# Another order for the opening of a fused attention and mixture-of-experts kernel

## The chip, the cores and the metric

The kernel runs on one core of one Trainium2 chip. The metric is the device time of one execution in microseconds (us), the median of several runs. TensorE multiplies matrices and also transposes tiles (a matmul with an identity matrix), VectorE and ScalarE do element-wise work, GpSimd (POOL) helps with setup and some subtractions, and SyncE (SP) issues DMAs.

## The reference

Three stages follow each other. The change lies in the first.

```python
q_bits = (einsum('bhsd,dk->bhsk', q, proj) > 0)     # 6 bits for each row; k_bits alike
mask = q_bucket[..., :, None] == k_bucket[..., None, :]
scores = scale * q @ k.T                            # 2 batches x 8 heads, 768 x 768, head size 64
scores = where(mask, scores, -1e9); scores -= max(scores, -1)
attn = exp(scores); attn /= sum(attn, -1) + 1e-9
x = (attn @ v), heads side by side                  # 1536 tokens x 512
x = (h * tanh(softplus(h))) @ w_out, h = x @ w_in   # 512 -> 2048 -> 512
out = one of 8 experts for each token, by cosine similarity: relu(x @ w1[e]) @ w2[e] * gate
```

## The kernel before, in words

There are 16 heads, numbered 0 to 15 through both batches. Each head goes through the same steps, and the later heads run side by side in a software pipeline whose step g does one sixth of a head. The opening, from the first load to the start of that pipeline, has an order of its own, which is written out by hand as the text `PRO`: each line names a step and its head. `run_all` walks over the lines and issues the instructions of each. A dependency is added between neighbours on each engine, so each engine runs its instructions in the order in which the lines issue them, and an instruction that must wait holds all that stand behind it on its engine.

The steps of the lines:

- `load_kq` (L276) loads k and q of two heads, one DMA of 384 KB each; `load_v` (L368) loads v of two heads, two DMAs of 192 KB. SP issues these in the opening, in program order. The line `kq 4` is the load of heads 4 and 5.
- `hi n` (L286): ScalarE rounds k and q of head n to a first float16 part, 768 columns. `lo n s` (L292): VectorE takes the second float16 part of k (s=0) or q (s=1). `lo_pool n` (L297, L301): the same for a whole head, with ScalarE scaling in place and GpSimd subtracting.
- `x n p`: twelve 128x128 transposes on TensorE (L254), into two PSUM tiles of pool p (s or o). `cx n 0` and `cx n 1` (L256) copy these two tiles to SBUF; the last letter names the engine, a for ScalarE and d for VectorE.
- `dup n` (L307) copies the first parts into the mask tile `kq` of the head. `args n` (L320): twelve small matmuls that project k and q on 6 directions, into PSUM (with `o`, into the pool that is also used by `x 1` and `m 1`). `bits n`, three times (L330, L331, L332): VectorE sums the projections and writes +-16384 by their sign into the mask tile; so a matmul of the mask tiles of q and k gives a large number where the buckets agree.
- `m n p` and `cm n 0`, `cm n 1`: twelve transposes of the mask tile and the copies of the results, like x and cx. They read all that dup and bits write.
- `max_unit n j c` finds the maximum of each row. With c=0: one matmul of 512 columns (L382) into a PSUM tile of the pool `ps_m`, and one VectorE reduction (L383). With c=1: two matmuls of 256 columns (L386), one reduction (L387). That pool has two buffers, so a unit's matmul waits until VectorE has read the unit before the last. For head 0 each unit with c=0 first issues one filler matmul (L230) into the same tile. A head needs nine units.
- `max_end n` (L395, L396): the two small VectorE operations that end the maxima. `rows_t n` (L403) transposes the maxima to a row, six small transposes, and `rows_in n` (L407) copies the row into the mask tile's 97th row.
- `score_unit n t`: four matmuls (L422 of q and k; L424 of the mask with the row of maxima) and one exponential on ScalarE (L427).
- `warm k` and `warm_s k` issue k filler matmuls (L230), whose results nobody reads.
- `pv` (L444), later in the pipeline, multiplies the exponentials by v.

The tiles that hold the first and second parts (`ka`) have two buffers, the mask tiles `kq` three, and the tiles that the loads write two, for two heads each.

Of the kernel before, what the change touches and what calls it, by code (L numbers as in the profile page):

```python
# [76 lines left out]
lo 1 0  # L77
m 0 s
lo 1 1
dup 1 d  # L80
cm 0 0 a
hi 2
cm 0 1 d
x 1 o
max_unit 0 0 0
kq 4
max_unit 0 1 1
cx 1 0 a
lo_pool 2
max_unit 0 3 0  # L90
cx 1 1 a
max_unit 0 2 0
warm_s 2
args 1 o 0
warm_s 5
args 1 o 1
bits 1
max_unit 0 1 0
max_unit 0 3 1
x 2 s  # L100
bits 1
cx 2 0 a
dup 2 a
max_unit 0 4 0
bits 1
max_unit 0 5 0
max_unit 0 5 1
m 1 o
cx 2 1 a
max_end 0  # L110
max_end 0
cm 1 0 a
max_end 0
rows_t 0
rows_in 0
args 2 m
bits 2
bits 2
bits 2
cm 1 1 a  # L120
hi 3
lo_pool 3
score_unit 0 0
max_unit 1 0 0
hi 4
# [22 lines left out]
class Attn:  # L148
# [364 lines left out]
    def run_all(self, bs, hook=None):  # L513

        seq = [(b, h) for b in bs for h in range(H)]
        N = len(seq)

        self.load_v(0, 0)
        self.load_kq(0, 2)
        act, dve = self.nc.scalar.copy, self.nc.vector.tensor_copy  # L520
        Z, pools, copies, its = self.Z, dict(s=self.ps_s, o=self.ps_o, m=self.ps_m), dict(a=act, d=dve), {}
        for line in PRO:
# [38 lines left out]
        for n in range(N):  # L561
            for name, at in AT.items():
# [10 lines left out]
                elif name in GAP:  # L573
                    d = GAP[name]
# [15 lines left out]
        for g in range(G0, TEND + 1):  # L590
            n, t = divmod(g, NJ)
            m, j = divmod(g + MXL, NJ)
# [848 lines left out]
```

## Time and profile before

| what | us |
|---|---|
| median of 3 runs | 677.6 (677.41 to 677.87) |
| the profiled execution | 676.44 |
| its span, first to last instruction | 674.5 |
| granted TensorE clock, mean | 0.998 of full speed |
| VectorE busy | 480.2 (71%) |
| ScalarE busy | 483.8 (72%) |
| GpSimd busy | 167.8 (25%) |

The times of rows are microseconds from the start of the span. A row of a timeline gives the start, how long the row lasted, the engine, the line of the kernel, the operation, the written tile, the read tile, and how many instructions were merged (x2). In brackets is how long the engine had been idle before it, and which instruction released it by the profile. Instructions of an engine overlap a little at their ends. PE is TensorE's matmuls, PEld its weight loads, DVE is VectorE and ACT ScalarE.

### The profile page before, as it was taken

The page shows a single profiled execution, that of the slowest core. Times are in us where ns is not written, and L with a number is a line of the kernel's source. Part 1 is how long each engine was busy: PE and PEld are TensorE (multiplying, and loading weights), DVE is VectorE, ACT ScalarE, POOL GpSimd, SP SyncE. Part 2 cuts the span into 40 slices and gives each one's busy share as a digit, 9 for nine tenths or more (in the row PEclk, how much of TensorE's full clock was granted, in tenths as well). Part 3 has the DMA queues.
Part 4 walks back from the last instruction along what each step waited for, and adds up shares of the span by engine and source line. Part 5 has one row for each costly group of instructions (what it writes and reads, how often), then busy time and mean ns, then how long its engine had stood idle before and what let it go on. Part 6 is the DMA issues. An engine that isn't in the chain of part 4 may idle for free. (4 is left out here: it accounts for less than half of the span.)

```text
span 674.5 us, 10665 instructions
## 1 busy us (share of the span) xinstructions
PE 657.5 (97%) x3946; PEld 376.9 (56%) x3946; DVE 480.2 (71%) x784; ACT 483.8 (72%) x735; POOL 167.8 (25%) x226
## 2 busy tenths in 40 slices
PE   7899999999999999999999999999999999999995
PEld 4555555555555544444444544445477777667772
DVE  6868999999988559999575676755565655556620
ACT  5657788787776889899799788887754655555530
POOL 4123132131231223222253242532522011101011
PEclk9999999999999999999999999999999999999999
DMA  7165675958663323457033030310355999989700
GB/s 234 33 152 115 181 180 118 235 135 181 158 124 88 87 63 103 115 178 207 15 85 89 1 126 13 84 31 1 127 187 179 258 280 309 293 249 262 179 23 22
DMA packets 119772, 92.72 MB, mean 137 GB/s; under 512 B 86788, under 2 KB 99076, under 8 KB 119714
## 3 DMA queue, kind: packets, MB, share of 16 engines
q1 hardware_dynamic: 111442, 80.65, 45.5%
q0 software_dynamic: 2240, 6.31, 3.3%
q10 hardware_dynamic: 6032, 5.01, 2.4%
q8 instruction: 33, 0.54, 0.4%
q14 instruction: 25, 0.20, 0.1%
HBM read 63.44 MB, written 14.24 MB: 115 GB/s over the span
## 5 line engine op out<-in xcount | busy, mean ns | idle before, releaser
L820 PE MATMUL h<-xx,wi 128*128 128x512 f16 x576 | 131.3, 379 | 0.7 <-DVE w L905 0.6
L879 PE MATMUL x<-wo,g 128*128 128x512 f16 x576 | 131.2, 379 | 0.0
L444 PE MATMUL o<-p,vn 128*65 128x384 f32 (+3 forms) x272 | 108.7, 486 | 0.3 <-ACT su L469 0.3
L427 ACT ACTIVATE p<-s 128x768 f32<-128x768 f32 x96 | 76.9, 806 | 31.5 <-PE s L424 30.1
L915 POOL TENSOR_TENSOR g<-w,g 128x512 f16<-128x512 f32 x47 | 57.7, 1228 | 149.2 <-ACT g L914 89.8
L879 PEld LDWEIGHTS <-g 128*128 128x128 f16 x576 | 56.3, 98 | 68.0 <-POOL g L915 0.3
L820 PEld LDWEIGHTS <-wi 128*128 128x128 f16 x576 | 56.1, 98 | 68.0 <-issue 1.7
L1220 PE MATMUL y<-b,hh 128*128 128x512 f16 (+1 forms) x384 | 84.2, 379 | 0.0
L1206 PEld LDWEIGHTS <-a 128*128 128x128 f16 x768 | 75.0, 98 | 5.6 <-issue 0.5
L383 DVE TENSOR_REDUCE mx<-ms 128x1 f32<-128x512 f32 x96 | 65.3, 686 | 8.1 <-PE ms L382 7.4
L1206 PE MATMUL h<-xt,a 128*128 128x240 f16 x672 | 70.3, 266 | 0.2 <-DVE hh L1213 0.2
L1220 PEld LDWEIGHTS <-hh 128*128 128x128 f16 (+1 forms) x384 | 43.7, 114 | 37.6
L921 DVE SCALAR_TENSOR_TENSOR w<-w,u 128x512 f32<-128x512 f32 x47 | 32.5, 691 | 45.3 <-ACT u L912 45.3
L704 DVE SCALAR_TENSOR_TENSOR b<-st,b 128x1024 f16<-128x1024 f32 x28 | 33.1, 1222 | 28.4 <-ACT b L703 28.4
L444 PEld LDWEIGHTS o<-p,vn 128*65 128x65 f32 (+1 forms) x272 | 42.3, 163 | 18.2 <-issue 8.0
L1226 POOL DMA_INDIRECT out_dram<-o,row x16 | 16.1, 1006 | 143.4 <-ACT o L1225 129.8
L704 DVE SCALAR_TENSOR_TENSOR a<-st,a 128x1024 f16<-128x1024 f32 x28 | 34.3, 1224 | 19.5 <-ACT a L703 19.1
L900 DVE SCALAR_TENSOR_TENSOR t<-t,u 128x512 f32<-128x512 f32 x47 | 40.6, 863 | 9.9 <-ACT t L927 9.9
L424 PE MATMUL s<-tm 97*128 97x384 f16 x192 | 47.0, 325 | 0.0
L422 PE MATMUL s<-tx 128*128 128x384 f16 x192 | 46.8, 325 | 0.0
L1225 ACT ACTIVATE o<-y,row 128x512 f32<-128x512 f32 (+1 forms) x16 | 11.0, 686 | 42.6 <-PE y L1220 22.8
L387 DVE TENSOR_REDUCE mx<-ms 128x2 f32<-128x512 f32 x48 | 32.9, 686 | 9.8 <-PE ms L386 9.1
(207 smaller groups left out, 1070.3 us busy)
## 6 DMA issues: line engine op xcount, KB each, us to landing
st<-in_moe_w_dram SPq DMA_DIRECT2D x32, 1024.0 KB, 6.3
stg<-in_moe_w_in_dram SPq DMA_DIRECT2D x16, 512.0 KB, 4.4
stg<-in_moe_w_out_dram SPq DMA_DIRECT2D x16, 512.0 KB, 4.2
xs<-zrow SPq DMA_DIRECT2D x15, 257.0 KB, 6.7
vn<-in_v_dram SPq DMA_DIRECT2D x16, 192.0 KB, 4.2
rb<-rd SPq DMA_DIRECT2D x14, 192.0 KB, 3.4
xr<-row SPq DMA_DIRECT2D x2, 1024.0 KB, 5.6
kq<-in_k_dram ACTq DMA_DIRECT2D x5, 384.0 KB, 4.4
```

Source lines behind the costliest of these rows:

```text
L383: nc.vector.tensor_reduce(z["mx"][:, j, 0:1], s, axis=AX.X, op=ALU.max)
L422: nc.tensor.matmul(s[:, c, :], kq[:, 0, ts], kq[:, 1, c * HS : (c + 1) * HS], start=True, stop=False)
L424: nc.tensor.matmul(s[:, c, :], m[0:97, 0, ts], m[0:97, 1, c * HS : (c + 1) * HS], start=False, stop=True)
L427: nc.scalar.activation(p[:, 0:S].rearrange("p (c n) -> p c n", c=2), s, AF.Exp, scale=2.0**-11)
L444: nc.tensor.matmul(o, self.vn(b, h, t), z["p"][t][:, cs], start=(t == 0), stop=(t == NJ - 1))
L704: nc.vector.scalar_tensor_tensor(lo, src, sc, hi, op0=ALU.mult, op1=ALU.subtract)
L820: self.nc.tensor.matmul(h, self.wi[wu][:, k, fs], x[:, k, xs], start=(i == 0), stop=(i == 3 * NKT - 1))
L879: nc.tensor.matmul(x2[r], gf[:, gu, rs], self.wo[wu][:, f, :], start=(f == 0 and gu + wu == 0), stop=(f == NF1 - 1 and gu == 1))
L900: nc.vector.scalar_tensor_tensor(t1, t1, 0.75, u1, op0=ALU.add, op1=ALU.mult)
L915: nc.gpsimd.tensor_tensor(g[G - 1][:, 1, :], p1, g[G - 1][:, 0, :], op=ALU.subtract)
L1206: nc.tensor.matmul(h[:, v, :], W[0][wu][:, k, fs], xt[e][:, xu * NKT + k, :], start=(i == 0), stop=(i == 3 * NKT - 1))
L1220: nc.tensor.matmul(y[s][0 : CS[s].stop - CS[s].start], hs[F // 2][:, hu, F % 2, CS[s]], W[1][wu][:, F, :], start=(F == 0 and hu + wu == 0) ...
```

## The change

The two loads of k and q of heads 2 and 3 are issued ahead of the two of v. In the opening, head 1's second copy `cx 1 1` goes ahead of head 2's split `hi 2` on ScalarE, and both ahead of `lo_pool 2`; head 1's `dup` on VectorE moves behind the first two maxima units. The seven fillers around head 1's projections become three, and both halves of these projections follow each other. The maxima of head 0, head 1's bits, head 1's mask transposes `m 1`, and head 2's transposes `x 2` are interleaved in another order: all three bits operations come before unit "4 0", `m 1` is before it on TensorE and `x 2` behind it. The split of head 3 (`hi 3`, `lo_pool 3`) is issued earlier, ahead of the last maxima of head 0, where it stood right before the first scores.

```diff
--- before.py
+++ after.py
@@ -77,49 +77,48 @@
 lo 1 0
 m 0 s
 lo 1 1
-dup 1 d
 cm 0 0 a
-hi 2
 cm 0 1 d
 x 1 o
 max_unit 0 0 0
 kq 4
 max_unit 0 1 1
 cx 1 0 a
+cx 1 1 a
+hi 2
+dup 1 d
 lo_pool 2
 max_unit 0 3 0
-cx 1 1 a
 max_unit 0 2 0
-warm_s 2
+warm_s 3
 args 1 o 0
-warm_s 5
 args 1 o 1
 bits 1
+dup 2 a
 max_unit 0 1 0
+bits 1
 max_unit 0 3 1
+bits 1
+hi 3
+m 1 o
+max_unit 0 4 0
+lo_pool 3
+cm 1 0 a
 x 2 s
-bits 1
+max_unit 0 5 0
 cx 2 0 a
-dup 2 a
-max_unit 0 4 0
-bits 1
-max_unit 0 5 0
 max_unit 0 5 1
-m 1 o
-cx 2 1 a
 max_end 0
 max_end 0
-cm 1 0 a
 max_end 0
+cx 2 1 a
 rows_t 0
 rows_in 0
+cm 1 1 a
 args 2 m
 bits 2
 bits 2
 bits 2
-cm 1 1 a
-hi 3
-lo_pool 3
 score_unit 0 0
 max_unit 1 0 0
 hi 4
@@ -515,8 +514,8 @@
         seq = [(b, h) for b in bs for h in range(H)]
         N = len(seq)
 
+        self.load_kq(0, 2)
         self.load_v(0, 0)
-        self.load_kq(0, 2)
         act, dve = self.nc.scalar.copy, self.nc.vector.tensor_copy
         Z, pools, copies, its = self.Z, dict(s=self.ps_s, o=self.ps_o, m=self.ps_m), dict(a=act, d=dve), {}
         for line in PRO:
```

## Rows read from the trace of the kernel before

**Rows 1.** The page, busy time: engine, us, share of the span, instructions.

```profile
PE 657.5 (97%) x3946; PEld 376.9 (56%) x3946; DVE 480.2 (71%) x784; ACT 483.8 (72%) x735; POOL 167.8 (25%) x226
```

**Rows 2.** Busy time by stretch: us, engines, then TensorE's granted clock, DMA share, GB/s.

```profile
5.00:10.00 5.00, 4.53 (x57) 3.15 (x56) 4.18 (x14) 2.27 (x3) 1.32 (x13) 1.00 0.89 262
...
18.00:19.00 1.00, 0.37 (x7) 0.19 (x4) 0.91 (x3) 0.93 (x2) 0.00 (x0) 1.00 0.19 66
...
20.00:25.00 5.00, 4.22 (x33) 2.39 (x32) 4.77 (x12) 4.97 (x8) 1.79 (x2) 1.00 0.00 0
...
35.00:40.00 5.00, 5.00 (x27) 2.44 (x27) 2.80 (x5) 3.33 (x5) 0.59 (x1) 1.00 0.79 205
```

**Rows 3.** Timeline of VectorE in the opening: start, us, instruction, idle time before.

```profile
9.44 0.36 DVE L307 COPY kq<-ka 128x768 f16<-128x768 f16 x1
...
11.36 0.68 DVE L387 TENSOR_REDUCE mx<-ms 128x2 f32<-128x512 f32 x1
...
14.81 0.38 DVE L330 TENSOR_REDUCE ag<-ar 128x72 f32<-128x216 f32 x1 [1.45 <-PE ar L320]
...
16.42 0.19 DVE L331 TENSOR_SCALAR kq<-ag 128x72 f16<-128x72 f32 x1
...
17.18 0.19 DVE L332 TENSOR_SCALAR kq<-ag 128x72 f16<-128x72 f32 x1
...
17.28 0.69 DVE L383 TENSOR_REDUCE mx<-ms 128x1 f32<-128x512 f32 x1
...
17.88 0.68 DVE L387 TENSOR_REDUCE mx<-ms 128x2 f32<-128x512 f32 x1
```

**Rows 4.** Timeline of TensorE's matmuls in the opening.

```profile
8.74 0.83 PE L254 MATMUL psm<-ident,kq 128*128 128x128 f16 x12 [0.24 <-DVE kq L332]
...
9.41 0.83 PE L254 MATMUL psx<-ident,ka 128*128 128x128 f16 x12
...
12.26 0.38 PE L382 MATMUL ms<-tm 96*128 96x512 f16 x1
...
12.47 0.49 PE L230 MATMUL warmed<-ones 128*128 128x384 f16 x2
...
14.47 0.31 PE L320 MATMUL ar<-pj,tx 128*128 128x18 f16 x6 [0.29 <-ACT tx L256]
...
14.63 0.32 PE L230 MATMUL ms<-ones 128*128 128x384 f16 x1
...
14.79 0.38 PE L382 MATMUL ms<-tm 96*128 96x512 f16 x1
...
19.03 0.50 PE L403 MATMUL tm<-ident,m 128*1 128x128 f16 x6 [0.66 <-DVE m L396]
...
20.18 0.48 PE L424 MATMUL s<-tm 97*128 97x384 f16 x2
...
23.51 0.38 PE L382 MATMUL ms<-tm 96*128 96x512 f16 x1 [0.57 <-DVE mx L387]
```

**Rows 5.** Timeline of ScalarE in the opening.

```profile
9.27 0.80 ACT L256 COPY tm<-psm 128x768 f16<-128x768 f16 x1 [1.21 <-PE psm L254]
...
11.45 0.84 ACT L286 ACTIVATE ka<-kq 128x768 f16<-128x768 f32 x1 [1.38 <-DVE mx L383]
...
13.62 0.79 ACT L256 COPY tx<-psx 128x768 f16<-128x768 f16 x1
...
20.34 0.84 ACT L297 ACTIVATE kq<-kq 128x768 f32<-128x768 f32 x1
...
21.09 0.79 ACT L427 ACTIVATE p<-s 128x768 f32<-128x768 f32 x1
```

**Rows 6.** SP's issue, its landing (last number, DMA view), v's first matmul.

```profile
6.03 0.47 SPq L276 DMA_DIRECT2D kq<-in_q_dram  x1
...
kq<-in_q_dram SPq DMA_DIRECT2D x1, 384.0 KB, 5.3
...
28.67 0.81 PE L444 MATMUL o<-p,vn 128*65 128x384 f32 x2
```

## The prediction

> **What bounds the kernel now.** I read the engine totals first. TensorE is busy for 97% of the span [rows 1], so a change of order pays only where TensorE stands idle, and nearly all of its idle time that this change can reach lies in the opening. Then I read the busy time by stretch [rows 2]: from 35 us on TensorE is busy in all of the five microseconds, while from 20 to 25 us it has 4.22 of 5.00 and VectorE 4.77. After that I read the timelines of the two engines, one beside the other. The reader is to see there who waits for whom. At 23.51 us a matmul of the maxima waited 0.57 us for a VectorE reduction [rows 4], because the two PSUM buffers of the maxima come free only when VectorE has read them. So between 20 us and the full stretch VectorE sets the pace, and it starts that work when the first head's row of maxima is done. That row is a chain: nine reductions, the two small operations that end them, six transposes on TensorE that start at 19.03 us, a copy, and the matmuls at 20.18 us that add the row to the first scores [rows 4]. Whatever moves these two times moves all that follows by as much, since from there on the order on each engine is the same, TensorE's and VectorE's work is the same, and TensorE fills up. The question of the change is thus when these transposes start. Inside the chain VectorE has one large hole, 1.45 us before 14.81 us, in which it waits for the second head's projections on TensorE [rows 3].
>
> **Part one: the loads.** The k and q loads of heads 2 and 3 are issued by SP ahead of the two v loads instead of behind them. Before, the later one (q) took 5.3 us from its issue at 6.03 us to land, at about 11.3 us [rows 6]. ScalarE's split of head 2 started at 11.45 us after 1.38 us of idling [rows 5]; the view names a VectorE reduction as releaser, but the split reads nothing of it, so I take the landing for the cause. With the new order the data is there earlier by the time of the two v loads. I cost this at nothing: in the new order ScalarE reaches that split only after two copies. The copy of head 0 starts at 9.27 us [rows 5]; one copy takes about 0.73 us start to start, so the two end near 11.5 us, which is where the split started before. The v loads now have two loads of 384 KB ahead of them; at the 262 GB/s of this stretch [rows 2] these take 3 us, and v lands later by so much. The first matmul that reads v runs at 28.67 us, more than 20 us after SP's issues here [rows 6], so the cover stays. If the cover were gone, the price would be that delay, at most 3 us. The next load on SP, of heads 4 and 5, waits for the second head's split on VectorE, which is not moved: nothing. The bounds for the part are 0 and -0.1 us.
>
> **Part two: the second head's copies on ScalarE go ahead.** Now both end near 11.5 us; before, the second started at 13.62 and ended at 14.41 us [rows 5]. So the projections of head 1 no longer wait for ScalarE; they wait for their place on TensorE. The matmul of the fourth maxima unit starts at 12.26, and the first filler behind it at 12.47 [rows 4]. Three fillers at 0.16 us each (14.63 to 14.79) put the projections at 12.95. All twelve now run together: their second six started at 14.47, lasted 0.31 us and had the next matmul start 0.16 us behind them [rows 4], so twelve take 0.31 us of issue and end near 13.41. On VectorE the copy named dup of head 1 has moved into the maxima: it lasts 0.36 us, of which I count 0.27, since an operation starts some 0.09 us before the one ahead of it ends (the reduction at 17.28 lasts 0.69, and the next starts 0.60 later) [rows 3]. Its place is free at about 11.97, a reduction after 11.36. So the next two reductions run at 12.24 and 12.84, and the first bits operation of head 1 can go at 13.45. That is 1.36 us earlier than 14.81, and the hole has closed. Bounds: 1.45 us at the best, nothing if the projections come no sooner.
>
> **Part three: the other order of the maxima.** Here the gain is spent again. After the projections TensorE issues a filler and the matmul of unit "1 0" at 13.42; it takes 0.38 us, so VectorE reduces it at 13.84 (before: projections 14.47, filler 14.63, matmul 14.79 [rows 4]). The second bits operation follows 0.60 us later, at 14.44. From the second bits operation to the third there were 0.76 us with one reduction between them (16.42 to 17.18) [rows 3], so the third starts at 15.20 and ends at 15.39. Now TensorE has the twelve mask transposes of head 1 as its next work, ahead of the matmul of unit "4 0", and they read what the third bits operation wrote. They start at about 15.45 and occupy TensorE for 0.67 us (8.74 to 9.41, where two such sets follow each other) [rows 4]. Only then come the filler at 16.12 and the matmul at 16.28, which VectorE can reduce at 16.70. VectorE could have gone on at 15.30 (0.10 behind the third bits operation, as at 17.18 and 17.28 [rows 3]) and has nothing until 16.70: a new hole of 1.40 us, counted from start to start. Behind that matmul (0.22 us of issue, as from 12.26 to 12.47 [rows 4]) stand head 2's twelve transposes, again 0.67 us, from 16.50 to 17.17. The matmul of unit "5 0" is at 17.33 and its reduction at 17.75, while VectorE was free at 17.31: a second hole of 0.44 us. The last reduction starts 0.60 later, at 18.35, against 17.88 before [rows 3]. From the start of that reduction to the row's transposes were 1.15 us (17.88 to 19.03), which puts them at 19.50. From there to the matmuls with the row were 1.15 us again (19.03 to 20.18) [rows 4], so they run at 20.65. The shift is +0.47 us.
>
> **Part four: what ScalarE and GpSimd gain.** The split of head 3 and its scaling leave the place right before the first exponential for the idle time after 13 us. The scaling at 20.34 held the first exponential until 21.09 [rows 5], when its scores had been done since 20.66 (20.18 and 0.48 [rows 4]). In the new order the scores are done at 21.13, and the exponential starts then: ScalarE's delay of 0.43 us goes, and the late row uses it up. Nothing on VectorE or TensorE waited for that exponential. I take zero, with 0 and -0.4 us as the bounds. Four fillers fewer save 0.65 us of TensorE's time, but they stood in waits; zero on the path.
>
> **The sum.** -1.36 (the projections earlier, with dup's 0.27 already in it), +1.40 and +0.44 (two new holes) make +0.48 us; the single starts above, rounded at each step, give 0.47. The profiled execution took 676.44 us, 1.94 of it outside its span of 674.5, and nothing outside the span changes, so it would become 676.9. The median of the runs shown is 677.6, 1.2 us more, and the same +0.5 gives 678.1 us. The ends: if VectorE never waited in the new order, the chain would gain 1.45 less dup's 0.27, or -1.2 us; if the projections came no earlier and both holes were paid, +1.8 us.
>
> **Rivals.** What a measurement of this kernel can tell from no change is about 0.2%, or 1.36 us.
> (a) The hole closes and none opens: the mask transposes run before VectorE runs out of reductions. It would need the third bits operation to end by about 14 us, and my times say 15.39. For it speaks the 1.45 us hole, against it the strict order on TensorE. Price -1.2, 676.4 us.
> (b) The opening shifts, but the later stretch takes it back: the ScalarE time of part four turns out to matter between 20 and 27 us. For it speaks that ScalarE was busy for 4.97 of 5.00 us there [rows 2], against it that TensorE's waits there name VectorE. Price 0, 677.6 us.
> (c) The clock falls. The new order leaves TensorE idle from about 14.0 to 15.45 and from 17.9 to 19.50 us, with four fillers fewer; before, its longest waits after the first matmul were 0.66 and 0.57 us [rows 4]. If the granted clock fell to its lower level (1.2 GHz, half) by 20 us, the 4.22 us of matmul time from 20 to 25 us would become 8.44 in place of 5.00: +3.4 us for each such stretch, 681.5 us with the shift. It decides as soon as one stretch behind the holes shows a clock under 1.00. Against it: from 18 to 19 us TensorE was busy for only 0.37 us, and the clock stayed at 1.00 [rows 2]. The Trainium skill's page "TensorE: Matmul & The Clock Gate", section "What's actually happening", speaks against the change here: "the default state is throttled, and activity releases the throttle". By that rule less activity in the opening is a risk; the trace of before, at 1.00 in all stretches read, shows no change of level.
> (d) The projections come late all the same, because the 'o' buffer or a semaphore holds them: +1.8, 679.4 us.
>
> **How the numbers follow.** Forecast 0.58, (a) 0.12, (b) 0.17, (c) 0.06, (d) 0.07. Forecast and (b) are within 0.2%. Of (a) half may pass the bound, with the scatter of the runs (677.41 to 677.87), so faster gets 0.06. (c) and most of (d) pass it on the other side: slower 0.12. The rest, 0.82, is no change that can be told. The range reaches to (a) and (d), 676.3 to 679.4 us; the forecast's own range is 677.7 to 678.6.
>
> **What would show it.** Right: the first bits operation of head 1 near 13.45 us, a VectorE hole of over a microsecond before the reduction of unit "4 0" near 16.7, a smaller one before "5 0", the row's transposes near 19.5, a clock of 1.00. Wrong: transposes of the row before 19.0, or a clock under 1.00 between 15 and 25 us, or the full TensorE stretch starting no later although the row is late.

## The result, and the profile after

The changed kernel is slower. Its median is 682.43 us (680.01 to 683.50, 6 runs) against 677.67 (677.21 to 678.41, 6 runs) of the kernel before, 4.8 us more. The ratio of the runs is 1.0060, with a 95% interval of 1.0045 to 1.0076, which is 3.1 to 5.2 us. The profiled execution of the changed kernel took 682.44 us, with a span of 680.2. The forecast of 678.1 and the range up to 679.4 were wrong. The time is near that of rival (c), the fall of the clock, which was put at 681.5 us and had got a chance of 0.06.

The page shows the totals and TensorE's granted clock in 40 slices of 17 us each. TensorE's busy share is what it was [rows 1]; the new thing is the second digit of the clock, a 7. (The last digit covers the end of the span, where TensorE runs out of work.)

```profile
PE 659.2 (97%) x3942; PEld 378.4 (56%) x3942; DVE 480.7 (71%) x784; ACT 483.8 (71%) x735; POOL 168.1 (25%) x226
...
PEclk9799999999999999999999999999999999999997
```

The same row of the kernel before:

```profile
PEclk9999999999999999999999999999999999999999
```

The busy time by stretch, as in [rows 2], shows where that is (the number behind POOL is the granted clock):

```profile
12.00:16.00 4.00, 2.38 (x23) 1.18 (x22) 3.99 (x8) 3.88 (x5) 1.78 (x2) 1.00 1.00 341
...
16.00:20.00 4.00, 3.43 (x30) 2.32 (x30) 1.60 (x5) 2.87 (x4) 1.85 (x2) 0.71 0.67 222
...
20.00:24.00 4.00, 2.93 (x24) 1.72 (x25) 2.20 (x8) 0.52 (x2) 0.23 (x1) 0.50 0.00 0
...
24.00:28.00 4.00, 3.43 (x28) 2.15 (x26) 3.66 (x7) 3.28 (x5) 0.05 (x1) 0.94 0.00 0
```

From 12 to 16 us TensorE was busy for 2.38 of 4.00 us, with the clock still at 1.00. In the next four the mean fell to 0.71, it was 0.50 (the level of 1.2 GHz) from 20 to 24 us, and it came back before 25 us. Taken together, that is some 7 us at the lower level.

The timeline of TensorE's matmuls answers to [rows 4]:

```profile
14.06 0.38 PE L385 MATMUL ms<-tm 96*128 96x256 f16 x2
...
16.28 0.84 PE L253 MATMUL psm<-ident,kq 128*128 128x128 f16 x12 [1.84 <-DVE kq L331]
...
17.12 0.38 PE L381 MATMUL ms<-tm 96*128 96x512 f16 x1
...
17.34 1.19 PE L253 MATMUL psx<-ident,ka 128*128 128x128 f16 x12
...
18.64 0.63 PE L381 MATMUL ms<-tm 96*128 96x512 f16 x1
...
21.07 0.80 PE L402 MATMUL tm<-ident,m 128*1 128x128 f16 x6 [1.36 <-DVE m L395]
...
22.73 0.85 PE L423 MATMUL s<-tm 97*128 97x384 f16 x2
...
26.84 0.38 PE L381 MATMUL ms<-tm 96*128 96x512 f16 x1 [0.57 <-DVE mx L386]
```

The twelve mask transposes of head 1 waited 1.84 us for the third bits operation. Behind them the matmul of unit "4 0" still took 0.38 us, but head 2's twelve transposes took 1.19 in place of 0.83, and a maxima matmul 0.63. That is the fall; it came behind the first wait, while TensorE was at work again, and before the second wait. The row's transposes waited another 1.36 us and ran at 21.07, the matmuls with the row at 22.73. The matmul that had waited at 23.51 us [rows 4] waited for the same reduction at 26.84: 3.33 us later. From there to the end of the attention stage nothing is gained or lost: the first matmul of the next stage starts at 240.69 us in place of 237.38, which is 3.31 us later.

The timeline of VectorE, as in [rows 3]:

```profile
11.17 0.69 DVE L382 TENSOR_REDUCE mx<-ms 128x1 f32<-128x512 f32 x1 [0.49 <-PE ms L381]
...
13.87 0.38 DVE L329 TENSOR_REDUCE ag<-ar 128x72 f32<-128x216 f32 x1
...
14.87 0.65 DVE L330 TENSOR_SCALAR kq<-ag 128x72 f16<-128x72 f32 x1
...
15.44 0.68 DVE L386 TENSOR_REDUCE mx<-ms 128x2 f32<-128x512 f32 x1
...
16.04 0.18 DVE L331 TENSOR_SCALAR kq<-ag 128x72 f16<-128x72 f32 x1
...
17.54 0.69 DVE L382 TENSOR_REDUCE mx<-ms 128x1 f32<-128x512 f32 x1 [1.32 <-PE ms L381]
...
19.32 0.69 DVE L382 TENSOR_REDUCE mx<-ms 128x1 f32<-128x512 f32 x1 [1.08 <-PE ms L381]
...
19.93 0.68 DVE L386 TENSOR_REDUCE mx<-ms 128x2 f32<-128x512 f32 x1
```

The two holes are there, 1.32 and 1.08 us. One thing is new: the second bits operation, at 14.87, took 0.65 us in place of 0.19. GpSimd's rows beside it:

```profile
13.69 1.78 POOL L300 TENSOR_TENSOR ka<-kq,ka 128x384 f16<-128x384 f32 x2 [7.39 <-ACT kq L296]
...
16.02 1.85 POOL L300 TENSOR_TENSOR ka<-kq,ka 128x384 f16<-128x384 f32 x2 [0.55 <-ACT kq L296]
```

The two subtractions of head 2 are the first row; they ended at 15.47 us, and the bits operation at 15.52.

ScalarE's split of head 2 came, as forecast, right behind the two copies, and no longer waited:

```profile
11.86 0.87 ACT L285 ACTIVATE ka<-kq 128x768 f16<-128x768 f32 x1
```

The list of TensorE's waits (total, times, longest) holds the rest:

```profile
PE psm L253 <- DVE kq L331: 2.1, 2, 1.8
...
PE tm L402 <- DVE m L395: 1.4, 1, 1.4
...
PE h L1205 <- DMA xt<-xs: 1.1, 2, 0.8
```

The first two lines are the opening. The third, 1.1 us for transposes by DMA, lies at 528 us in the expert stage. It is not among the waits of before, but stands in all profiles below with 0.4 to 1.2 us, also where the time is that of before, so I do not count it to the change. So 3.3 of the 5.7 us between the two spans come from the opening; the rest is this wait and the last output write.

To compare profiles I use one number: from the start of the first maxima reduction to the row's transposes. It leaves out when the first reduction starts, which differs between executions (10.20 to 11.25 us in the profiles here). Before: 10.75 to 19.03, 8.28 us. After: 11.17 to 21.07, 9.90 us.

### The profile page after: what moved, and what is told of

Its sections match the earlier page's. It is cut to its first block, busy times and chain, and to the rows that moved or that the text cites. A ratio compares the mean times of both kernels' runs of the same rounds, so it can differ in the third digit from the quotient of the medians.

```text
span 680.2 us, 10656 instructions
## 1 busy us (share of the span) xinstructions
PE 659.2 (97%) x3942; PEld 378.4 (56%) x3942; DVE 480.7 (71%) x784; ACT 483.8 (71%) x735; POOL 168.1 (25%) x226
```

## The experiments

Each kernel was timed against the kernel before on the same chip. "Low" counts the runs whose mean granted clock over the span was 0.994 or less; of 82 runs of the kernel before beside them there were 7. This is a rough sign. The mean also takes in the end of the span, where a lower clock costs nothing (the granted clock was 0.67 from 670 to 675 us in the profile of before, with TensorE idle). And it can miss a fall in the opening: the profiled run of e7 has 0.995 and is not counted, though its clock fell to 0.63. The "row" column is the number just described, from the one profile of each.

| kernel | us | ratio to before, 95% | low | row, us |
|---|---|---|---|---|
| the change | 682.43 | 1.0060 (1.0045 to 1.0076) | 6 of 6 | 9.90 |
| e1 loads alone | 677.22 | 0.9990 (0.9978 to 1.0002) | 0 of 11 | 7.77 |
| e2 order alone | 682.52 | 1.0067 (1.0050 to 1.0085) | 6 of 6 | 12.05 |
| e3 change, both waits filled | 679.26 | 1.0020 (1.0008 to 1.0031) | 1 of 12 | 9.18 |
| e4 early copies alone | 678.06 | 1.0002 (0.9989 to 1.0014) | 2 of 12 | 7.93 |
| e5 change, mask transposes late | 678.03 | 0.9992 (0.9980 to 1.0004) | 0 of 12 | 8.08 |
| e6 change, first wait filled | 680.20 | 1.0028 (1.0013 to 1.0042) | 4 of 12 | 9.18 |
| e7 change, second wait filled | 679.87 | 1.0029 (1.0014 to 1.0043) | 5 of 12 | 10.51 |
| e8 waits filled, GpSimd later | 681.44 (one run) | | | 8.78 |
| e9 mask transposes early, alone | 681.07 | 1.0043 (1.0027 to 1.0060) | 4 of 7 | 9.68 |
| e10 bits together | 677.41 | 0.9995 (0.9983 to 1.0008) | 0 of 12 | 7.09 |
| e11 before, seven fillers out | 678.63 | 1.0020 (1.0006 to 1.0033) | 7 of 12 | 7.92 |

**e1, the loads alone.** The two lines of `run_all` in the new order, in the kernel before.

```diff
-        self.load_v(0, 0)
         self.load_kq(0, 2)
+        self.load_v(0, 0)
```

> The kernel before with only the k and q loads of heads 2 and 3 moved ahead of the v loads. Clock theory (the change is slower because TensorE's hole ahead of head 1's mask transposes lets the clock fall): the loads open no hole, so 677.2 to 678.2 us, all stretches up to 40 us at 1.00 after the first rise. Loads theory (the earlier k and q, or the later v, disturb the opening): a good part of the 4.8 us shows here, 679 us or more.

No loss shows: 0.9990, an interval with 1 in it. The split of head 2 started after 0.88 us of idling in place of 1.38 [rows 5], and its releaser is now named as the load of q, so it had waited for the landing:

```profile
10.54 0.84 ACT L286 ACTIVATE ka<-kq 128x768 f16<-128x768 f32 x1 [0.88 <-DMA kq<-in_q_dram]
```

The landing also moves the row number. In ScalarE's old order head 1's second copy stands behind this split. The split started 0.70 us after the first reduction in the profile of before and 0.20 here, 0.50 less, and the row came 0.51 us sooner. In e11, with the loads as before, the split started 0.35 us after it and the row came 0.36 sooner. So the 8.28 us of before are those of one execution with a late landing, and a row that is shorter by up to half a microsecond need not be the work of an edit.

**e2, the order alone.** The changed `PRO` with the loads as before.

```diff
-        self.load_kq(0, 2)
         self.load_v(0, 0)
+        self.load_kq(0, 2)
```

> The changed kernel with the loads as before, so the new order of the opening alone. Clock theory: like the changed kernel, 680.5 to 683.5 us, with about 7 us at half clock from 17 or 18 us on. Loads theory: close to before, under 679 us.

It is as slow as the whole change, with the clock low in all six runs. The loads are out. Its first wait was longer than that of the change, since both bits operations took long in it, 0.81 and 0.94 us (the reason is shown in e8):

```profile
16.23 1.46 PE L253 MATMUL psm<-ident,kq 128*128 128x128 f16 x12 [2.75 <-DVE kq L331]
```

**e3, both waits filled.**

```diff
 hi 3
+warm_s 10
 m 1 o
...
 max_unit 0 5 1
+warm_s 8
 max_end 0
```

> The changed kernel with ten fillers ahead of head 1's mask transposes and eight behind the last maxima matmul of head 0, so that TensorE's two long waits are filled with work that nobody reads. Clock theory: 1.00 throughout after the first rise, VectorE's two holes stay, and the time is 678.0 to 679.2 us. Chain theory (the holes on VectorE and what follows from them cost the time whatever the clock does): 680.5 us or more, with the clock at 1.00.

Of the 4.8 us, 1.25 are left; the median is 0.06 us above the range of the clock theory and below that of the chain theory. Its stretches stay at 1.00, and the fillers' rows show that they fill (start, us):

```profile
16.00:20.00 4.00, 3.81 (x38) 2.62 (x38) 2.28 (x6) 3.00 (x4) 1.77 (x2) 1.00 0.64 215
...
20.00:24.00 4.00, 3.85 (x44) 2.47 (x44) 3.16 (x9) 1.78 (x3) 0.28 (x1) 1.00 0.00 0
```

```profile
14.19 1.81 PE L231 MATMUL warmed<-ones 128*128 128x384 f16 x10
...
18.63 1.47 PE L231 MATMUL warmed<-ones 128*128 128x384 f16 x8
...
20.25 0.50 PE L404 MATMUL tm<-ident,m 128*1 128x128 f16 x6
...
24.73 0.38 PE L383 MATMUL ms<-tm 96*128 96x512 f16 x1 [0.56 <-DVE mx L388]
```

At 24.73 the matmul waits that stood at 23.51 before, so the shift is 1.22 us; 0.32 of it were there at the first reduction (11.07 against 10.75), and 0.90 are the chain's. In the profile of the change the shift is 3.33, of which 0.42 were there at the first reduction. So with the chain's 0.90 taken off, the slow stretch cost 2.01 us in that execution. The 0.90 are counted from the one profile of before; counted from the row of e11, 7.92, they would be 1.26.

**e4, the early copies alone.** Copies, dup and three fillers as in the change; the rest as before.

```diff
-dup 1 d
 cm 0 0 a
-hi 2
...
 cx 1 0 a
+cx 1 1 a
+hi 2
+dup 1 d
 lo_pool 2
 max_unit 0 3 0
-cx 1 1 a
 max_unit 0 2 0
-warm_s 2
+warm_s 3
 args 1 o 0
-warm_s 5
 args 1 o 1
```

> The kernel before with only the second head's copies ahead of the third head's split, dup of head 1 behind two maxima units, and three fillers in place of seven; maxima, bits, mask transposes and head 3's split keep the order of before. Clock theory: no hole over 1 us on TensorE, clock at 1.00, VectorE's hole of 1.45 us gone and none new, row transposes 0.7 to 1.2 us earlier than before and the time 676.4 to 677.2 us. Fewer-fillers theory (four fillers less are enough for the clock to fall): 679 us or more.

No gain in time, against what I expected, and no fall in the profile (2 of 12 runs are low): the three fillers are not the cause by themselves. In the profile the row came 0.35 us sooner, not 0.7 to 1.2, since head 2's transposes waited twice for GpSimd, 0.39 and 0.36 us. The matmul that waited at 23.51 us before did so at 22.71 here, but later matmuls of the attention stage waited for transposes by DMA, such as 0.39 us at 126.55 and 0.47 at 165.88, and the next stage began 0.13 us later than before. Weight loads that wait 0.5 us or more for such a transpose stand in the profiles of e2 and of e4 to e9, in no other; I take them for scatter.

**e5, mask transposes late.** The change, with head 1's mask transposes and their copies behind the maxima.

```diff
 hi 3
-m 1 o
 max_unit 0 4 0
 lo_pool 3
-cm 1 0 a
 x 2 s
 max_unit 0 5 0
 cx 2 0 a
 max_unit 0 5 1
+m 1 o
+cx 2 1 a
 max_end 0
 max_end 0
+cm 1 0 a
 max_end 0
-cx 2 1 a
```

> The changed kernel, but head 1's mask transposes issued behind all maxima matmuls of head 0, where they stood before; nothing else is put back. Hole theory (the transposes that wait for the third bits operation hold the maxima and open the hole in which the clock falls): no TensorE wait over 1 us after the first matmul, clock at 1.00 from the first rise to 40 us, VectorE without a hole over 0.5 us in the maxima, row transposes 0.8 to 1.4 us earlier than before, time 676.3 to 677.6 us against 677.7 to 678.0 for before. Rival (the early copies, dup and three fillers are enough for the fall, or the earlier split of head 3 costs time): 679 us or more.

The whole loss is gone: 0.9992, no low run. So the place of the mask transposes is what makes the change slow. The gain that I expected did not come. Here both bits operations are long, 0.65 and 0.94 us, and eat most of it (the last row is GpSimd's, beside the second of them):

```profile
14.87 0.65 DVE L330 TENSOR_SCALAR kq<-ag 128x72 f16<-128x72 f32 x1
...
16.04 0.94 DVE L331 TENSOR_SCALAR kq<-ag 128x72 f16<-128x72 f32 x1
...
18.10 0.67 DVE L386 TENSOR_REDUCE mx<-ms 128x2 f32<-128x512 f32 x1
...
16.01 1.78 POOL L300 TENSOR_TENSOR ka<-kq,ka 128x384 f16<-128x384 f32 x2 [0.55 <-ACT kq L296]
```

TensorE was busy for 2.52 of 4.00 us from 16 to 20 us, but its longest wait there was 0.92 us, and the clock stayed at 1.00:

```profile
16.00:20.00 4.00, 2.52 (x39) 1.78 (x37) 3.34 (x8) 2.92 (x4) 1.78 (x2) 1.00 0.69 228
```

**e6 and e7, one wait filled.** In e6 only `warm_s 10`, in e7 only `warm_s 8` of e3.

> The changed kernel with ten fillers in the first long wait of TensorE alone (ahead of head 1's mask transposes). If the first hole makes the clock fall: as with both filled, 678.5 to 679.7 us, clock at 1.00. If the second wait, ahead of the row's transposes, does as much: 680.5 us or more in the median, with the clock low behind 20 us.

> The changed kernel with eight fillers in the second long wait alone (behind the last maxima matmul of head 0). If the first hole makes the clock fall: 681 to 683 us, with the clock low from 15 to 18 us on. If the second does: 678.5 to 679.7 us.

Neither theory is right: each wait by itself lets the clock fall in some executions. 4 and 5 of 12 runs are low, and at least one more of e7 fell, its profiled run; with both waits open, all 12 runs of the change and of e2 are low. The clock in the profile of e6 fell behind the second wait, that of e7 behind the first:

```profile
16.00:20.00 4.00, 2.58 (x31) 1.85 (x30) 2.28 (x6) 2.93 (x4) 1.85 (x2) 1.00 0.78 266
...
20.00:24.00 4.00, 3.66 (x34) 2.44 (x35) 2.75 (x8) 1.61 (x3) 0.28 (x1) 0.67 0.00 0
```

```profile
16.00:20.00 4.00, 3.93 (x32) 2.95 (x33) 1.24 (x3) 2.72 (x4) 1.66 (x2) 0.63 0.66 227
...
20.00:24.00 4.00, 4.00 (x42) 2.34 (x41) 2.96 (x10) 1.15 (x3) 0.28 (x1) 0.94 0.00 0
```

**e8, GpSimd out of the way.** e3 with head 2's scaling, subtraction and transposes moved back, and with `cm 1 1` moved forward; the last lines only let `dup 2` run ahead of `lo_pool 2`.

```diff
-lo_pool 2
 max_unit 0 3 0
...
 max_unit 0 4 0
-lo_pool 3
 cm 1 0 a
-x 2 s
+lo_pool 2
+lo_pool 3
 max_unit 0 5 0
-cx 2 0 a
+cm 1 1 a
...
 rows_in 0
-cm 1 1 a
+x 2 s
+cx 2 0 a
+cx 2 1 a
...
-        del z["kq32"]
+        if b * H + h != 2:
+            del z["kq32"]
```

> The changed kernel with both waits filled, and with head 2's scaling, GpSimd subtraction and transposes moved behind head 1's mask transposes, so that GpSimd is idle while VectorE does head 1's bits. If GpSimd's subtraction holds VectorE's bits operation: the second bits operation lasts 0.20 us in place of 0.65, and the mask transposes start 0.4 to 0.5 us earlier after the first bits operation than in the version with fillers alone. If not (the operation is long for another reason): 0.65 us again. The total is not of interest, since head 2's transposes now come late.

The bits operations take 0.19 us, and the mask transposes start 2.06 us after the first of them in place of 2.42 in e3, 0.36 us sooner where 0.4 to 0.5 were expected. The third bits operation came 0.48 us sooner, but the ten fillers ahead of the transposes ran on a little behind it. The hold has moved with GpSimd: it now runs four pieces of 0.91 us from 17.57 us on, and there the small operation that ends the maxima takes 0.59 in place of 0.17.

```profile
14.35 0.19 DVE L333 TENSOR_SCALAR kq<-ag 128x72 f16<-128x72 f32 x1
...
15.05 0.19 DVE L334 TENSOR_SCALAR kq<-ag 128x72 f16<-128x72 f32 x1
...
18.78 0.59 DVE L398 TENSOR_SCALAR m<-m 128x6 f16<-128x6 f32 x1
```

```profile
17.57 3.52 POOL L302 TENSOR_TENSOR ka<-kq,ka 128x384 f16<-128x384 f32 x4 [11.32 <-ACT kq L298]
```

**e9, mask transposes early, alone.**

```diff
 max_unit 0 3 1
-x 2 s
 bits 1
-cx 2 0 a
-dup 2 a
-max_unit 0 4 0
 bits 1
+m 1 o
+max_unit 0 4 0
+cm 1 0 a
+x 2 s
 max_unit 0 5 0
+cx 2 0 a
+dup 2 a
 max_unit 0 5 1
-m 1 o
-cx 2 1 a
 max_end 0
 max_end 0
-cm 1 0 a
+cx 2 1 a
```

> The kernel before with one part of the change alone: head 1's second and third bits operations together behind unit "3 1", and head 1's mask transposes ahead of unit "4 0", with head 2's transposes behind it. Loads, copies, dup, all seven fillers and head 3's split stay as before. Hole theory: TensorE waits 1.2 to 1.6 us ahead of the mask transposes and about as long ahead of the row's, the clock falls behind one of them in most runs, 680.5 to 683.5 us. Rival (the three fillers or the early copies are needed for the fall): clock at 1.00 and 678 to 679.5 us from VectorE's holes alone.

This part alone makes the kernel before slower by 3.3 us, with all seven fillers in place. The four low runs took 681.07 to 681.99 us, the other three 679.19 to 680.01, which is still over the 677.80 of before: the new holes cost time without the clock, and the clock adds to it. The two waits, and the stretch behind them:

```profile
16.86 0.84 PE L254 MATMUL psm<-ident,kq 128*128 128x128 f16 x12 [1.38 <-DVE kq L332]
...
20.93 0.50 PE L403 MATMUL tm<-ident,m 128*1 128x128 f16 x6 [1.57 <-DVE m L396]
```

```profile
20.00:24.00 4.00, 3.08 (x27) 1.73 (x28) 2.48 (x8) 3.83 (x6) 0.92 (x2) 0.71 0.00 0
```

**e10, bits together.** The change with the order that the runs pointed to (and `dup` as in e8).

```diff
 dup 1 d
-lo_pool 2
+dup 2 a
...
 bits 1
-dup 2 a
-max_unit 0 1 0
+lo_pool 2
 bits 1
-max_unit 0 3 1
 bits 1
-hi 3
+max_unit 0 1 0
+max_unit 0 3 1
 m 1 o
 max_unit 0 4 0
-lo_pool 3
 cm 1 0 a
-x 2 s
 max_unit 0 5 0
-cx 2 0 a
+cm 1 1 a
 max_unit 0 5 1
+x 2 s
+cx 2 0 a
...
 rows_in 0
-cm 1 1 a
...
 bits 2
+hi 3
+lo_pool 3
```

> The changed kernel's loads and early copies, with head 1's three bits operations right behind each other, head 2's scaling behind the first of them (so GpSimd starts when they are done), the mask transposes behind unit "3 1", head 2's transposes behind all maxima, and head 3's split as late as before. If the holes and GpSimd's hold are the whole cost of the change's order: no VectorE hole over 0.3 us between the first bits operation and the row, bits operations of 0.2 us, row transposes 1.0 to 1.5 us earlier than before counted from the first reduction, clock at 1.00, time 676.4 to 677.2 us. Rival (an early row is not passed on, or the clock falls in another place): 677.6 us or more.

In the trace it does what was expected. The bits operations are short, VectorE goes on without a hole, and the row comes 1.19 us sooner than in the profile of before, 0.83 sooner than in that of e11:

```profile
13.86 0.38 DVE L330 TENSOR_REDUCE ag<-ar 128x72 f32<-128x216 f32 x1
...
14.28 0.20 DVE L331 TENSOR_SCALAR kq<-ag 128x72 f16<-128x72 f32 x1
...
14.39 0.19 DVE L332 TENSOR_SCALAR kq<-ag 128x72 f16<-128x72 f32 x1
...
17.11 0.68 DVE L387 TENSOR_REDUCE mx<-ms 128x2 f32<-128x512 f32 x1
```

In the profiles this is passed on: the next stage began 0.84 us sooner than before, although the first reduction came 0.41 later. The median, 677.41 against 677.80, lies between the two ranges that were expected, and the interval has 1 in it. So the version does not show as faster than before; a gain of 0.4 us would be below what these runs can tell.

**e11, no fillers.** The kernel before without them.

```diff
-warm_s 2
 args 1 o 0
-warm_s 5
 args 1 o 1
```

> The kernel before without the seven fillers around head 1's projections, and nothing else. If the removed fillers alone let the clock fall: 680 us or more in the median, clock low behind 15 us. If a wait that is longer than the one that they filled is needed: TensorE waits about 1.1 us ahead of the second half of the projections, the clock holds, and the time is 677.4 to 678.6 us.

The time is between the two: 0.8 us slower, and low in 7 of 12 runs, four of them at 0.994 exactly. The profiled run is not one of these; its clock is at 1.00 through the opening, and its longest wait there is this one:

```profile
13.97 0.31 PE L318 MATMUL ar<-pj,tx 128*128 128x18 f16 x6 [1.12 <-ACT tx L254]
```

Where the clock fell in the low runs, no trace shows.

## Why the prediction was wrong

**The step that failed** is the price of the two waits on TensorE. The sum counted the holes that the mask transposes open as VectorE's time alone, +1.40 and +0.44 us, and put what they could do to TensorE's clock at nothing. Rival (c) named both waits and the fall, but was put at 0.06, because TensorE had once been busy for only 0.37 us of a microsecond while the clock stayed. One such microsecond, whose longest wait was 0.66 us, was no bound for waits of 1.84 and 1.36 us. The runs show what stands in its place: the order alone is slow (e2), with the mask transposes put back the loss is gone (e5), put early by themselves they bring most of it (e9), and with 18 fillers in the two waits, which compute nothing, the clock stays and the time is 679.26 in place of 682.43 us (e3). The four fillers that were taken out, which the sum put at "zero on the path", are not this step: with three in place of seven and no new wait, e4 shows no loss. Only with none at all, in e11, is there one of 0.8 us.

The price of (c), 3.4 us, was near in its total: from the change to e3 it is 3.2 us by the medians and 2.7 by the ratios, with about 1 us of uncertainty in each, and 2.0 in the one pair of profiles. The working behind it does not hold, so this is partly luck: it was one stretch of five microseconds at half clock, and the profile shows some 7 us at the lower level for those 2.0.

**The loads** were right: no cost (e1), and the split in the new order waits for the copies alone. **The early copies** were right to the hundredth against the profile that they were worked out from: from the first reduction to the first bits operation there were 4.06 us before and 2.70 after, 1.36 less. That part of the 4.06 was the late landing was not seen: e1, e9 and e11, with the copies as before, have 3.56 to 3.71 us, and against these the gain is about 1 us. The sum also has a slip here: its best end, -1.2 us, is smaller than the term of -1.36 that it should bound, because the hole was taken as idle time in the one and from start to start in the other.

**The holes** were right in kind and place, and the chain was late by more than forecast. The third bits operation was to come 1.75 us after the first and came after 2.17; the reduction of unit "4 0" was to come after 3.25 and came after 3.67. Both differ by 0.42 us, and the term that was mis-sized is the second bits operation, put at the 0.19 us of a row where GpSimd stood still [rows 3]. Beside GpSimd's subtraction it takes 0.65 (e8 takes the cause away). So the chain at full clock is 0.90 us late in place of 0.47, and e3's time, 0.5 to 2.1 us over before by its interval, is in line with it. The second hole, put at 0.44, was 0.36 us in e3 and 1.08 at the low clock:

```profile
18.50 0.69 DVE L384 TENSOR_REDUCE mx<-ms 128x1 f32<-128x512 f32 x1 [0.36 <-PE ms L383]
```

**ScalarE's gain** shows nowhere, as forecast: with the mask transposes put back (e5) the earlier split of head 3 brings no gain in time. No run tests it by itself. It had a price that the forecast did not have: in e5 its GpSimd subtraction is what stands beside the bits operation of 0.94 us. Rival (a) fell with the two holes. Rival (b), that the later stretch takes the shift back, fell: the 3.33 us at 26.84 stayed to the end of the attention stage. Rival (d) fell as well, since the projections came in time.

What stays open: how much of 1.25 us in e3 is scatter, why a given execution falls behind one wait or the other, and where the clock fell in the low runs that have no profile.

## What to carry to other kernels

Filler matmuls in a wait cost nothing on the path as long as they end before the wait does (the row of e3 is that of e6, 9.18 us, with and without fillers in the second wait), but they may carry the clock: before removing fillers or opening waits like those of the change, price the work behind them at half clock and give that case a real chance. Transposes that need the last step of another engine's chain should not stand in TensorE's order ahead of the matmuls that feed that engine. And a short VectorE operation is short only as long as GpSimd is not at work beside it: take its duration from a row with the same neighbour.

## What the runs showed of the hardware

A VectorE operation of 0.19 us that started during a GpSimd subtraction lasted until that subtraction ended: 0.65 us in the change (to 15.52, the subtraction to 15.47), 0.94 us in e5 (to 16.98, the first of two to 16.92), and 0.59 us for the operation of 0.17 us in e8 (to 19.37, the second of four to 19.35). The reductions of PSUM beside the same subtractions kept 0.68 to 0.69 us. In the change the third bits operation, started at 16.04 with GpSimd's row at 16.02, was not held (0.18 us), and the subtraction took 0.98 in place of 0.91 us; in e5, at 16.04 and 16.01, it was held (0.94). The Trainium skill's page "SBUF — State Buffer", section "Who interferes with whom", states that VectorE in some modes and GpSimd share a pair of ports, which whoever issues first holds for its whole instruction while the other waits. The traces agree with their 0.65, 0.94 and 0.59 us. Which mode these operations ran in, no run here shows.

The first matmuls also come up to speed at another time in each profile. Head 0's first twelve transposes, at 5.89 us in both profiles, took 0.93 us before and 1.49 after, though TensorE's work ahead of them is the same. I read this as the lower level lasting longer, since the fillers ahead of them start 0.32 us apart and those behind them 0.16 us; the granted clock in these stretches does not show it, it reads 1.00. With it the first reduction starts 0.42 us later in the profile of the change. I take this to be part of the scatter of single runs.
